# Two products on zeros between the score blocks of each group in batch 0

## The chip, the cores and the metric

The kernel runs on one core of one Trainium2 chip. The metric is the device time of one execution in microseconds; "before" is the median of four executions. A profiled execution has a span, from its first to its last instruction, and its own device time, which is a little longer.

## The reference

Attention over 8 batches of 12 heads (448 positions, 64 values a head), and then a two-layer network on its output.

```python
def _attn_ref(q, k, v):                       # each (8, 12, 448, 64)
    scores = q @ k.T / sqrt(64)
    attn = softmax(scores)
    return attn @ v

def _moe_ref(x, w_in, w_out):                 # x (3584, 768)
    h = x @ w_in                              # (3584, 2048)
    g = np.maximum(0.01 * h, h)
    return g @ w_out                          # (3584, 768)
```

## The kernel before

The work is cut into groups: a group `u` is two heads of one batch, so there are 48 groups, six to a batch (`HP` is 6). A group's path is this. `load` (line 91) fetches q, k and v; `cast` (104) turns them into bfloat16, on GpSimd except in group 0; `transposes` (164) turns q and k by eight TensorE products with the identity into PSUM (line 170), and VectorE copies them out (173). From group 12 on, a DMA does the turning.

`scores` (177) computes one block of 112 keys against all 448 queries, for both heads: two products of 64 rows into one slot of the pool `ps_s`. A group has four such blocks, c = 0 to 3. The pool has two slots, so that a block has to wait until the exponential of the block two before it has read its slot. `expo` (189) takes the exponential of a block on ScalarE (line 191), 112 partitions by 896 elements. `pv` (193) computes one head's product with v: 16 products (line 200) into the single slot of `ps_pv`, then a reciprocal (207) and a multiply (208) on VectorE. `x_transposes` (212) turns the result into `xT`, which the two-layer network reads.

`mlp` (236) is that network, over the tokens of one batch: products with `w_in` (line 243), the activation on ScalarE (248), products with `w_out` (260), a copy (265) and the store.

The order of the work is written out by hand: a schedule of eight slots for each group (`slots`, 306), in which each engine executes its instructions in the order in which they are issued. In slot 0 the first two blocks of scores are issued, in slot 2 the first head's `pv` of the group before, in slot 3 the transposes of the group after, in slot 4 the last two blocks, in slot 6 the second head's `pv` of the group before. For TensorE a steady group of batch 0 is therefore: blocks 0 and 1, the x transposes of two groups before, 16 pv products, 8 transposes, blocks 2 and 3, 16 pv products. Batch 0 (groups 0 to 5) has no network to run beside it. Group 6 has slots of its own (`turning_slots`, 271): it finishes batch 0 before it goes on. From slot 3 of group 6 on, the products of a batch's network are put between the slots of the next batch, in proportion.

`warm_up` (133) issues products of a tile of zeros with itself, 128 rows by 512 columns, each into a slot of `ps_mm`, the pool of two slots that the network uses later. Nothing reads what they write. Before, there are nine at the start (line 138), two after the first transposes (361) and four in slot 0 of group 0 (316), behind its two blocks.

Of the kernel before, what the change touches and what calls it, by code (L numbers as in the profile page):

```python
# [16 lines left out]
def kernel(  # L17
# [14 lines left out]
    HP = H // 2  # L32
# [58 lines left out]
    def load(u, queues=(nc.sync,) * 3):  # L91
        if u >= NU:
            return
        b, hp = divmod(u, HP)
        raw[u] = []
        for a, name, eng in zip((q, k, v), ("fq", "fk", "fv"), queues):
            t = ld_pool.tile([SC, 2, NSC, D], F32, name=name)
            eng.dma_start(
                out=t.rearrange("p h so d -> p h (so d)"),
                in_=a[b, 2 * hp:2 * hp + 2].rearrange("h (p so) d -> p h (so d)", so=NSC),  # L100
            )
            raw[u].append(t)

    def cast(u, by=(nc.gpsimd.tensor_copy,) * 3):
        if u >= NU:
            return
        fq, fk, fv = raw.pop(u)
        qk_sb[u] = cast_pool.tile([SC, 2, NSC, 2, D], BF16, name="qkb")
        by[0](qk_sb[u][:, 0].rearrange("p so h d -> p h so d"), fq)  # L109
        by[1](qk_sb[u][:, 1].rearrange("p so h d -> p h so d"), fk)  # L110
        by[2](v_sb[u % NV][:, :, :, :D], fv)  # L111
# [8 lines left out]
    def load_w(n=1):  # L120
        for _ in range(n):
            if w_steps:
                o, i = w_steps.pop(0)
                nc.gpsimd.dma_start(out=o, in_=i)  # L124
# [8 lines left out]
    def warm_up(n):  # L133
        for _ in range(n):
            ps = ps_mm.tile([P, 512], F32, name="mm")
            nc.tensor.matmul(ps, warm[:, :P], warm, start=True, stop=True)  # L136
# [23 lines left out]
    def dma_transposes(u):  # L160
        if NPE <= u < NU:
            turn(qkT[u % NQ][:, :QL], qk_sb[u].rearrange("p i so h d -> p (i so h d)"))

    def transposes(u):
        if u >= min(NPE, NU):
            return
        tr = ps_tr.tile([P, 2, S], BF16, name="tr")
        for i in range(2):
            for so in range(NSC):
                nc.tensor.transpose(  # L170
                    tr[:, i, ts(so, SC)], qk_sb[u][:, i, so], ident[:SC, :SC]
                )
        nc.vector.tensor_copy(qkT[u % NQ][:, :QL], tr.rearrange("p i s -> p (i s)"))  # L173
# [3 lines left out]
    def scores(u, c):  # L177
        ps = ps_s.tile([P, 2, 512], F32, name="sc")
        t = qkT[u % NQ]
        sc_t[u, c] = ps  # L180
        for j in range(2):
            nc.tensor.matmul(  # L182
                ps[:, j, :S],
                t[j * D:(j + 1) * D, S + c * SC:S + c * SC + P],
                t[j * D:(j + 1) * D, :S],
                start=True, stop=True,
            )

    def expo(u, c):
        e = e_sb[u % NE][:, :EL].rearrange("p (j c s) -> p j c s", j=2, c=NSC)  # L190
        nc.scalar.activation(e[:, :, c, :], sc_t.pop((u, c))[:SC, :, :S], AX.Exp, scale=scale)  # L191

    def pv(u, j):

        e, vt = e_sb[u % NE], v_sb[u % NV]
        ps = ps_pv.tile([P, NSC, D + 1], F32, name="pv")
        for qc in range(NSC):
            for c in range(NSC):
                at = (j * NSC + c) * S + qc * SC
                nc.tensor.matmul(  # L200
                    ps[:, qc, :], e[:, at:at + P], vt[:, j, c, :],
                    start=(c == 0), stop=(c == NSC - 1),
                )
        if j == 0:
            x_t[u] = x_pool.tile([SC, NSC, 2, D], BF16, name="x")
        rec = r_pool.tile([SC, NSC, 1], F32, name="rec")
        nc.vector.reciprocal(rec, ps[:SC, :, D:])  # L207
        nc.vector.tensor_mul(  # L208
            x_t[u][:, :, j, :], ps[:SC, :, :D], rec.to_broadcast([SC, NSC, D])
        )  # L210

    def x_transposes(u):
        b, hp = divmod(u, HP)
        at = b * S % NX
        dst = xT[:, hp, at:at + S]
        if u >= NPE - 3:
            turn(dst, x_t.pop(u).rearrange("p so h d -> p (so h d)"))
            return
        tr = ps_tr.tile([P, 2, S], BF16, name="tr")
        for so in range(NSC):  # L220
            nc.tensor.transpose(tr[:, 0, ts(so, SC)], x_t[u][:, so], ident[:SC, :SC])  # L221
        nc.vector.tensor_copy(dst, tr[:, 0, :])  # L222
# [83 lines left out]
    def slots(u):  # L306

        on = u < NU

        def s0():  # L310
            if on:
                scores(u, 0)
                scores(u, 1)
                expo(u, 0)
            if u == 0:
                warm_up(4)

        def s1():
            if on:
                expo(u, 1)  # L320
            if 2 <= u <= NU + 1 and u - 2 not in (HP - 2, HP - 1):
                x_transposes(u - 2)
            dma_transposes(u + 2)

        def s2():
            if 1 <= u <= NU:
                pv(u - 1, 0)

        def s3():
            load(u + 5)  # L330
            load_w({2: 1, 3: 2, 4: 2, 5: 2}.get(u, 0))
            if u + 1 < NU and u + 1 != HP:
                transposes(u + 1)

        def s4():
            if on:
                scores(u, 2)
                scores(u, 3)
                expo(u, 2)

        def s5():
            if on:
                expo(u, 3)
            cast(u + 3)

        def s6():
            if 1 <= u <= NU:
                pv(u - 1, 1)

        def s7():  # L350
            pass

        return [s0, s1, s2, s3, s4, s5, s6, s7]

    steps = [s for u in range(NU + 2) for s in (turning_slots if u == HP else slots)(u)]
# [53 lines left out]
```

## Time and profile before

| | |
|---|---|
| device time, median of 4 executions | 428.53 us (425.99 to 432.26) |
| the profiled execution, device time | 429.24 us |
| its span | 427.5 us |
| mean granted TensorE clock | 0.988 |
| score products (line 182) | 384, 55.0 us busy |
| exponentials (line 191) | 192, 168.1 us busy, 916 ns each |
| products on zeros (line 136) | 15, 5.3 us busy |

Batch 0 lies in the first 28 us or so of the profile, the turn to the dense part up to about 35 us; from there on TensorE has the network's products. "PE" is TensorE's products, "PEld" its weight loads, ACT ScalarE, DVE VectorE, POOL GpSimd. The granted clock is a share of full speed. [...]

### The profile page before, as it was taken

To read this page: it belongs to the slowest core of one execution; us is meant where nothing else is said; L and a number is where in the kernel's file an instruction comes from. 1 tells how busy PE (TensorE), PEld (TensorE's weight loads), DVE (VectorE), ACT (ScalarE), POOL (GpSimd) and SP (SyncE) were. 2 spreads that over 40 slices of the span, in tenths; PEclk is the share of its full clock that TensorE was granted. 3 is DMA by queue.
4 is the path that set the end of the run, shared out by engine and by line. 5 is a ranking of instruction groups with operands and counts; after the bars stand their busy time and mean duration, and the time that the engine had idled before them with its cause. 6 is when DMAs were issued, how large, how long until landed. Compare 5 with 4: busy or idle time off the path is not lost.

```text
span 427.5 us, 8982 instructions
## 1 busy us (share of the span) xinstructions
PE 414.3 (97%) x3716; PEld 227.8 (53%) x3731; DVE 100.3 (23%) x271; ACT 230.2 (54%) x322; POOL 92.5 (22%) x168
## 2 busy tenths in 40 slices
PE   7979999999999999999999999999999999999995
PEld 2654665544555555544455555554455555654563
DVE  1542333221132212221122212221123211320021
ACT  5875774566634676457644476456753477314300
POOL 5593323222111222211221131221112100000000
PEclk9897999999999999999999999999999999999999
DMA  8999999984655966675374966686445440230022
GB/s 230 264 250 244 250 248 203 239 222 109 110 143 156 203 135 172 177 185 139 97 146 126 184 181 136 183 189 157 127 100 135 115 93 13 60 85 2 0 75 74
DMA packets 98505, 63.66 MB, mean 149 GB/s; under 512 B 55456, under 2 KB 94880, under 8 KB 98464
## 3 DMA queue, kind: packets, MB, share of 16 engines
q1 hardware_dynamic: 90928, 56.56, 55.3%
q0 software_dynamic: 7296, 6.29, 9.3%
q8 instruction: 29, 0.48, 0.5%
q10 hardware_dynamic: 240, 0.23, 0.2%
q14 instruction: 12, 0.10, 0.1%
HBM read 45.61 MB, written 11.01 MB: 132 GB/s over the span
## 4 chain that ended last, share of the span: by engine, by line
PE 94%; ACT 2%; DMA 1%; issue 1%; POOL 1%; DVE 1%; SPq 0%; ACTq 0%
PE mm L243 35%; PE mm L260 35%; PE pv L200 11%; PE sc L182 10%; ACT e L191 2%; PE tr L170 1%; DMA fv<-in_v_dram 1%; PE tr L221 0%; POOL w_in_sb L124 0%; DVE x L208 0%; DVE qkT L173 0%; POOL qkb L109 0%; POOL v L111 0%; POOL qkb L110 0%; DVE o L265 0%
## 5 line engine op out<-in xcount | busy, mean ns | idle before, releaser
L191 ACT ACTIVATE e<-sc 112x896 bf16<-112x896 f32 x192 | 168.1, 916 | 109.9 <-PE sc L182 109.7
L243 PE MATMUL mm<-xT,w_in_sb 128*128 128x384 bf16 (+1 forms) x753 | 161.3, 354 | 0.8
L260 PE MATMUL mm<-w_out_sb,h 128*128 128x384 bf16 x896 | 160.7, 326 | 0.0
L260 PEld LDWEIGHTS <-h 128*128 128x128 bf16 x896 | 81.4, 98 | 62.3 <-issue 14.5
L243 PEld LDWEIGHTS <-w_in_sb 128*128 128x128 bf16 x768 | 68.5, 98 | 71.4 <-issue 17.5
L248 ACT ACTIVATE h<-mm 128x384 bf16<-128x384 f32 (+1 forms) x128 | 69.9, 546 | 59.0 <-PE mm L243 59.0
L111 POOL CAST v<-fv 112x512 bf16<-112x512 f32 x48 | 29.7, 619 | 202.2 <-PE pv L200 174.0
L200 PEld LDWEIGHTS <-e 112*128 112x128 bf16 x1536 | 61.8, 98 | 16.6 <-DVE x L208 2.0
L207 DVE RECIPROCAL rec<-pv 112x4 f32<-112x4 f32 x96 | 17.6, 183 | 212.1 <-PE pv L200 211.7
L200 PE MATMUL pv<-v,e 112*128 112x65 bf16 x1536 | 65.7, 195 | 1.4 <-DVE x L208 1.4
L182 PE MATMUL sc<-qkT 64*128 64x448 bf16 x384 | 55.0, 360 | 3.9 <-ACT e L191 2.8
L265 DVE COPY o<-mm 128x384 f32<-128x384 f32 x56 | 31.2, 557 | 86.6 <-PE mm L260 86.4
L208 DVE TENSOR_TENSOR x<-pv,rec 112x256 bf16<-112x256 f32 x96 | 40.8, 425 | 3.6 <-DVE rec L207 0.3
L109 POOL CAST qkb<-fq 112x512 bf16<-112x512 f32 x47 | 29.0, 618 | 33.6 <-DMA fq<-in_q_dram 16.7
L110 POOL CAST qkb<-fk 112x512 bf16<-112x512 f32 x47 | 29.0, 617 | 10.7 <-DMA fk<-in_k_dram 10.2
L182 PEld LDWEIGHTS <-qkT 64*128 64x128 bf16 x384 | 12.0, 94 | 35.9 <-issue 30.6
L173 DVE COPY qkT<-tr 128x896 bf16<-128x896 bf16 x12 | 7.5, 622 | 7.2 <-PE tr L170 7.0
L170 PE MATMUL tr<-ident,qkb 112*128 112x112 bf16 x96 | 8.2, 234 | 0.2
L170 PEld LDWEIGHTS <-qkb 112*128 112x128 bf16 x96 | 6.7, 109 | 2.3 <-DVE qkb L109 0.4
L136 PE MATMUL mm<-warm 128*128 128x512 bf16 x15 | 5.3, 501 | 1.2 <-DVE warm L131 1.2
L222 DVE COPY xT<-tr 128x448 bf16<-128x448 bf16 x9 | 3.5, 391 | 9.3 <-PE tr L221 9.3
L221 PE MATMUL tr<-ident,x 112*128 112x112 bf16 x36 | 3.5, 222 | 0.7 <-DVE qkT L173 0.7
(17 smaller groups left out, 15.1 us busy)
## 6 DMA issues: line engine op xcount, KB each, us to landing
fq<-in_q_dram SPq DMA_DIRECT2D x48, 224.0 KB, 3.9
fv<-in_v_dram SPq DMA_DIRECT2D x48, 224.0 KB, 4.1
fk<-in_k_dram SPq DMA_DIRECT2D x47, 224.0 KB, 3.7
w_in_sb<-in_moe_w_in_dram POOLq DMA_DIRECT2D x4, 768.0 KB, 14.1
w_out_sb<-in_moe_w_out_dram POOLq DMA_DIRECT2D x4, 768.0 KB, 34.1
out_dram<-o SPq DMA_DIRECT2D x8, 336.0 KB, 3.0
out_dram<-o SPq DMA_DIRECT2D x8, 288.0 KB, 2.7
out_dram<-o SPq DMA_DIRECT2D x8, 240.0 KB, 3.2
```

The costliest lines, as they stand in the source:

```text
L109: by[0](qk_sb[u][:, 0].rearrange("p so h d -> p h so d"), fq)
L110: by[1](qk_sb[u][:, 1].rearrange("p so h d -> p h so d"), fk)
L111: by[2](v_sb[u % NV][:, :, :, :D], fv)
L170: nc.tensor.transpose(tr[:, i, ts(so, SC)], qk_sb[u][:, i, so], ident[:SC, :SC])
L182: nc.tensor.matmul(ps[:, j, :S], t[j * D:(j + 1) * D, S + c * SC:S + c * SC + P], t[j * D:(j + 1) * D, :S], start=True, stop=True,)
L191: nc.scalar.activation(e[:, :, c, :], sc_t.pop((u, c))[:SC, :, :S], AX.Exp, scale=scale)
L200: nc.tensor.matmul(ps[:, qc, :], e[:, at:at + P], vt[:, j, c, :], start=(c == 0), stop=(c == NSC - 1),)
L208: nc.vector.tensor_mul(x_t[u][:, :, j, :], ps[:SC, :, :D], rec.to_broadcast([SC, NSC, D]))
L243: nc.tensor.matmul(ps[:, :n], w_in_sb[:, kk, ts(m, P)], xT[:, kk, at:at + n], start=(kk == 0), stop=(kk == KD - 1),)
L248: nc.scalar.activation(h[:, m, :n], ps[:, :n], AX.Prelu, alpha=0.01)
L260: nc.tensor.matmul(ps[:, :NW], h[:, m, ts(c, P)], w_out_sb[:, m, ts(w, NW)], start=(m == 0), stop=(m == MD - 1),)
L265: nc.vector.tensor_copy(o[c][:, ts(w, NW)], ps[:, :NW])
```

## The change

In slot 0 and in slot 4 of groups 0 to 5, two products on zeros are issued between the two blocks of scores. The four products on zeros at the end of slot 0 of group 0 are taken out. In all there are 35 products on zeros instead of 15.

```diff
         def s0():
             if on:
                 scores(u, 0)
+                if u < HP:
+                    warm_up(2)
                 scores(u, 1)
                 expo(u, 0)
-            if u == 0:
-                warm_up(4)
...
         def s4():
             if on:
                 scores(u, 2)
+                if u < HP:
+                    warm_up(2)
                 scores(u, 3)
                 expo(u, 2)
```

## The prediction

> **What bounds the kernel now.** I read the page's PE, clock and chain lines first, then the busy time in stretches of about 3.41 us, then PE's and ACT's rows in order of time for batch 0.
>
> ```profile
> PE 414.3 (97%) x3716; PEld 227.8 (53%) x3731; DVE 100.3 (23%) x271; ACT 230.2 (54%) x322; POOL 92.5 (22%) x168
> ...
> PEclk9897999999999999999999999999999999999999
> ...
> PE 94%; ACT 2%; DMA 1%; issue 1%; POOL 1%; DVE 1%; SPq 0%; ACTq 0%
> ```
>
> TensorE is busy 97% of the span and carries 94% of the chain, so a microsecond gained or lost ahead of the dense part, which begins near 35 us, should reach the end. The change touches only batch 0. What can be won there is waits and clock; the clock line is below 9 in two slices only, and the stretches show why (columns: stretch, its length, then the busy time of PE, PEld, DVE, ACT, POOL, then the granted clock, DMA share, GB/s):
>
> ```profile
> 7.68:11.10 3.42, 2.05 (x23) 1.00 (x22) 0.62 (x1) 3.01 (x4) 2.67 (x5) 1.00 1.13 273
> 11.10:14.50 3.40, 3.40 (x46) 2.41 (x43) 1.25 (x4) 2.45 (x4) 2.04 (x4) 0.50 1.17 243
> ...
> 24.74:28.15 3.41, 2.56 (x46) 1.74 (x44) 1.67 (x6) 3.40 (x5) 3.41 (x6) 1.00 1.19 246
> 28.15:31.56 3.41, 2.05 (x46) 1.59 (x46) 1.68 (x6) 1.61 (x2) 3.41 (x6) 1.00 1.17 242
> 31.56:34.97 3.41, 2.70 (x30) 1.66 (x27) 1.62 (x4) 0.20 (x1) 1.45 (x3) 0.50 1.18 244
> 34.97:38.39 3.42, 3.42 (x19) 1.75 (x19) 0.62 (x1) 2.02 (x3) 0.72 (x3) 0.50 1.18 249
> ```
>
> Twice a stretch in which PE was busy 2.05 us (60%) is followed by half clock: 3.4 us of it at the start of the groups, and 6.8 us at the turn from batch 0 to the dense part. A stretch with 2.56 us (75%) is not. So the limit lies between 60% and 75%. Now one steady group (start, duration, engine; in brackets the idle time before the row and what ended it):
>
> ```profile
> 20.35 0.55 PE L182 MATMUL sc<-qkT 64*128 64x448 bf16 x4
> 20.83 0.69 PE L200 MATMUL pv<-v,e 112*128 112x65 bf16 x16
> 21.78 0.36 PE L182 MATMUL sc<-qkT 64*128 64x448 bf16 x2 [0.26 <-DVE rec L207]
> 22.59 0.36 PE L182 MATMUL sc<-qkT 64*128 64x448 bf16 x2 [0.44 <-ACT e L191]
> 22.89 0.37 PE L221 MATMUL tr<-ident,x 112*128 112x112 bf16 x4
> 23.09 0.67 PE L200 MATMUL pv<-v,e 112*128 112x65 bf16 x16
> ...
> 20.81 3.34 ACT L191 ACTIVATE e<-sc 112x896 bf16<-112x896 f32 x4 [0.54 <-PE sc L182]
> ```
>
> The four exponentials take 3.34 us, ACT then idles 0.54 us until the third block's scores, and the next group's third block starts at 24.22: a group takes 3.88 us. Its cycle is: third block's scores (20.35), exponential at 20.81, the next one, then the slot for the next group's second block at 22.59, and 1.63 us of PE work up to 24.22. PE waits 0.44 us between the first and second block of a group. Between its third and fourth block it waits for nothing: both come in one row at 20.35.
>
> **The change part by part.** *The order.* PE gets 24 products in place of 4; DVE, ACT, POOL and SP keep their instructions and order, and no DMA is moved. The number of uses of the two mm slots stays odd (35 for 15), so the first real product meets the same slot.
>
> *Price of a pair at full clock.* From these rows (starts: second score pair 6.49, first zeros product 6.77, the third 7.22 as 6.77+2x0.22):
>
> ```profile
> 6.49 0.35 PE L182 MATMUL sc<-qkT 64*128 64x448 bf16 x2
> 6.77 0.61 PE L136 MATMUL mm<-warm 128*128 128x512 bf16 x2
> ...
> 6.77 1.04 PE L136 MATMUL mm<-warm 128*128 128x512 bf16 x4
> ...
> 7.65 0.84 PE L170 MATMUL tr<-ident,qkb 112*128 112x112 bf16 x8
> ```
>
> Four products fill 7.65-6.77 = 0.88 us, 0.22 each. From a score pair to the first zeros product is 0.28 us, where the next score pair would come after 0.20. So a pair moves the block behind it from 0.20 to 0.28+0.44 = 0.72 us: 0.52 us late unless PE would have waited anyway. The step back from zeros to scores has no row; zeros to transposes costs nothing beyond the 0.22, transposes to scores about 0.1 (0.145 against 0.05 between transposes). I take 0, the row after a zeros product being the nearer; the upper end is 0.1 per pair. Below nothing this step can't go.
>
> *Pair between first and second block (steady).* 21.78+0.28+0.44 = 22.50, and the slot comes at 22.59: hidden with 0.09 to spare, if the first block itself starts on time.
>
> *Pair between third and fourth block.* The fourth block goes from 20.55 to 21.07; its exponential starts at 21.63 and needs about 0.41 us from the scores' start (8.42 to 8.83 in another group): hidden. But the 16 products behind it start 0.52 late, at 21.35, and reach their last at 21.84 (0.49 in). The next first block then comes at about 21.98 instead of 21.78, its pair ends at 22.70, and the second block is 0.11 to 0.13 late. Everything up to the next third block follows, so a steady group takes 4.01 instead of 3.88. Who waits: the reciprocal and multiply behind these 16 products also come 0.52 later, at 22.30 to 22.72, ahead of the transposes of x at about 23.02; hidden.
>
> *First groups.* In group 0 the removed four ended at 7.65, where the transposes were waiting only for POOL's second cast half 0.5 us later; the new pair moves the second block to 7.02, and its exponential is due at 7.51: nothing. With the two new pairs, the stretch 7.68 to 11.10 gets 0.88 us more PE work, 2.9 of 3.42 us (86%), above the limit, so the half clock of 11.10 to 14.50 should go. Without it: second block of group 1 at 10.60 as now (its pair ends at 9.79+0.72 = 10.51), 16 products from 10.90 to 11.39, transposes to 11.90, third block at 12.04 instead of 12.52: 0.48 us won.
>
> *Sum up to the turn.* Third block of group 1: 12.04 (-0.48). Group 2: 12.04+4.01 = 16.05 (16.53 now, -0.48, since that cycle was slow already). Group 3: 20.06 (20.35, -0.29). Group 4: 24.07 (24.22, -0.15). Group 5, without transposes behind it: +3.35+0.13 = 27.55 (27.57, -0.02). There the fourth block now waits until 28.08 and would start at 28.27, so the 16 products behind it are 0.19 late, their multiply too, and the next ones, which wait for it (0.82 us at 29.89), start at 30.08. The turn is +0.19 us. Supplies are in time: the casts of group 4's q and k end at 18.02, wanted at about 19.5.
>
> *The turn.* No pair stands after 28.3. PE still waits 0.82, 0.54 and 0.71 us between 29 and 34 us, so the half clock of 31.56 to 38.39 stays.
>
> So 0.2 us more than the profiled execution's 429.24 us, which is its 427.5 span and 1.7 around it: 429.4. That execution is 0.7 above the median, 428.53. Executions in which the first drop doesn't happen have nothing to win and pay 0.19+0.48 = 0.67. I take the middle, 0.43, on the median: 429.0.
>
> [...] The trace has no PE wait longer than 0.82 us in the stretch before the first drop, and the clock halves all the same at 11.10. [...]
>
> **The rivals.**
> - *The turn keeps its clock too.* If the stretches fall otherwise over the waits of 0.82, 0.54 and 0.71 us, none may reach the limit. Half clock from 31.56 to 38.39: 16 products at 0.054 instead of 0.033 apart and 8 transposes about 0.7 together, x transposes and scores 0.55, seven products of 0.16 more each 1.1, eight transposes 0.4, scores 0.15: 2.9 us. Time 426.1. Against it: the waits lie on a chain of DVE and ACT which no pair fills.
> - *Zeros don't hold the clock.* The first drop stays, and two pairs fall into it: zeros products at half clock are 0.43 apart (nine in 3.62 us at the start), so 2x(0.86+0.1) = 1.9 us, with 0.6 from the later groups: 431.0. Against it: the same zeros precede full speed from 5.4 us on.
> - *Slower than 1%: half clock through batch 0.* If the clock falls at 11.1 and does not return until the turn, a group is PE's alone: 4 score pairs 1.5, 32 products 1.7, 12 transposes 1.1, four zeros 1.7, changes 0.5: 6.6 us against 3.9. Four groups cost 10.9: 439.4. It decides from 1.6 such groups. Against it: before, 3.4 us of full PE work brought the clock back at 14.50.
> - *It does nothing to be seen:* the second and fourth term cancel; this is what the main case amounts to.
>
> **How the numbers follow.** Main case 0.62 (429.0; own range 427.5 to 430.5: the 0.48 may be 0 to 0.75, the step back to scores adds up to 0.1 on each of nine pairs); turn keeps its clock 0.17; zeros don't hold it 0.16; half clock throughout 0.05. The four runs before spread from 425.99 to 432.26, so the range is 426.0 to 432.0, leaving out the last case and the tails. About 1% (4.3 us) is what a measurement of this kernel can tell from no change: faster by more 0.03, within 0.91, slower by more 0.06 (half clock throughout, and the tail of the third).
>
> **What would show it.** Right: full clock from 4.3 us to the turn; PE without waits of 0.44 in batch 0; third blocks 4.0 apart; fourth blocks 0.72 behind third ones; half clock only around 32 to 38 us. Wrong: half clock inside batch 0; groups over 4.2 us apart (then the step from zeros to scores costs more than taken); no half clock at the turn (then 426).

## The result, and the profile after

The changed kernel takes 429.52 us (median of 53 executions, 427.65 to 431.34) against 428.28 us before (79 executions, 425.94 to 432.26): the ratio is 1.0026, with a 95% interval of 1.0015 to 1.0037. So it is slower by about a quarter of a per cent, 1.1 us by the ratio.

The profiled execution of the changed kernel took 427.88 us with a span of 426.1, which is less than the profiled one before (429.24 and 427.5). That is chance, and the page's lines say what kind of chance:

```profile
PE 415.5 (98%) x3733; PEld 226.8 (53%) x3751; DVE 100.1 (23%) x271; ACT 230.7 (54%) x322; POOL 92.9 (22%) x168
...
PEclk9999999999999999999999999999999999999999
...
PE 96%; DMA 1%; DVE 1%; POOL 1%; issue 0%; ACT 0%; SPq 0%
```

No slice has half clock, neither in batch 0 nor at the turn. The one before had 10.2 us of it. A single pair of profiles therefore compares two draws of the clock as well as two kernels; the row of one steady group compares the kernels (PE in order of time, then ACT's row):

```profile
20.54 0.36 PE L182 MATMUL sc<-qkT 64*128 64x448 bf16 x2
21.06 0.38 PE L136 MATMUL mm<-warm 128*128 128x512 bf16 x1 [0.16 <-issue]
21.37 0.36 PE L182 MATMUL sc<-qkT 64*128 64x448 bf16 x2
21.66 0.69 PE L200 MATMUL pv<-v,e 112*128 112x65 bf16 x16
22.28 0.36 PE L182 MATMUL sc<-qkT 64*128 64x448 bf16 x2
22.58 0.61 PE L136 MATMUL mm<-warm 128*128 128x512 bf16 x2
23.11 0.36 PE L182 MATMUL sc<-qkT 64*128 64x448 bf16 x2
23.41 0.37 PE L221 MATMUL tr<-ident,x 112*128 112x112 bf16 x4
23.62 0.67 PE L200 MATMUL pv<-v,e 112*128 112x65 bf16 x16
...
24.75 0.36 PE L182 MATMUL sc<-qkT 64*128 64x448 bf16 x2
```

```profile
21.00 3.50 ACT L191 ACTIVATE e<-sc 112x896 bf16<-112x896 f32 x4 [0.72 <-PE sc L182]
```

The third block starts at 20.54 and the next one at 24.75: a group takes 4.21 us where it took 3.88. PE's waits for a slot are gone (the 0.16 ahead of 21.06 is where the record of the pair's first product is missing), and ACT now idles 0.72 us a group instead of 0.54, waiting for PE. PE has become the bound of batch 0. From block to block with a pair between is 0.83 us, at both places (20.54 to 21.37, 22.28 to 23.11), where the prediction had 0.72.

At the turn PE waits three times, 1.2 us later than in the profile before. First the kernel before, whose third wait fell into half clock, then the changed one:

```profile
29.89 0.67 PE L200 MATMUL pv<-v,e 112*128 112x65 bf16 x16 [0.82 <-DVE x L208]
...
31.30 0.89 PE L200 MATMUL pv<-v,e 112*128 112x65 bf16 x16 [0.54 <-DVE x L208]
...
33.65 0.53 PE L221 MATMUL tr<-ident,x 112*128 112x112 bf16 x4 [0.71 <-DVE qkT L173]
```

```profile
31.07 0.67 PE L200 MATMUL pv<-v,e 112*128 112x65 bf16 x16 [0.82 <-DVE x L208]
...
32.48 0.69 PE L200 MATMUL pv<-v,e 112*128 112x65 bf16 x16 [0.54 <-DVE x L208]
...
34.43 0.36 PE L221 MATMUL tr<-ident,x 112*128 112x112 bf16 x4 [0.87 <-DVE qkT L173]
```

The waits are still there, and yet these stretches, of which the last two are cut at the 3.41 us grid on which the clock changed (last section), show that the clock held this time (columns as in the prediction):

```profile
8.60:28.66 20.06, 19.41 (x253) 10.61 (x254) 9.30 (x26) 17.30 (x20) 13.16 (x21) 1.00 1.15 249
28.66:32.08 3.42, 2.45 (x42) 1.50 (x40) 1.36 (x6) 1.80 (x3) 3.42 (x6) 1.00 1.18 243
32.08:35.49 3.41, 2.14 (x34) 1.53 (x35) 2.17 (x6) 0.31 (x1) 2.06 (x4) 1.00 1.18 245
```

The grid here cuts the turn's waits into two stretches with PE busy 72% and 63%; in the profile before it put two of them into one stretch with 60%, and the clock fell.

The mean granted clock of each execution tells how often that happens. One stretch of 3.41 us at 0.50 takes 0.004 off the mean of a span of 426 us, so an execution at 0.996 or less is counted as one with half clock; 0.997 to 0.999 can come from the clock's fall behind the last product, which in this profile stands at 424.62 us and gives 0.998. Of the 54 executions of the changed kernel with a clock on record 29 had half clock, and none is under 0.989; of the 93 executions of the kernel before that were taken beside the experiments 70 had it, down to 0.988.

The price alone shows in the executions without half clock. The fastest are 427.65 and 425.95 us, 1.7 apart, but the medians are 428.06 (25 executions) and 427.54 (23), only 0.5 apart: those of the changed kernel lie between 427.65 and 428.89, those of the kernel before spread from 425.95 to 429.75, for a reason that is not the clock and that stays open. With half clock the medians are 430.25 and 428.58. So the changed kernel has half clock less often, but loses more to it where it has it. The mean of all executions lies above the mean of those without half clock by 1.1 us in the changed kernel and by 1.0 us in the one before: a gain from the clock in the sum is not shown.

### The profile page after: what moved, and what is told of

It is laid out like the page before. It is cut to its first block, busy times and chain, and to the rows that moved or that the text cites. A ratio compares the mean times of both kernels' runs of the same rounds, so it can differ in the third digit from the quotient of the medians.

```text
span 426.1 us, 9019 instructions
## 1 busy us (share of the span) xinstructions
PE 415.5 (98%) x3733; PEld 226.8 (53%) x3751; DVE 100.1 (23%) x271; ACT 230.7 (54%) x322; POOL 92.9 (22%) x168
## 4 chain that ended last, share of the span: by engine, by line
PE 96%; DMA 1%; DVE 1%; POOL 1%; issue 0%; ACT 0%; SPq 0%
PE mm L260 35%; PE mm L243 35%; PE pv L200 12%; PE sc L182 11%; PE mm L136 1%; PE tr L170 1%; DMA fv<-in_v_dram 1%; PE tr L221 1%; DVE x L208 0%; ACT e L191 0%; POOL w_in_sb L124 0%; POOL qkb L109 0%; POOL v L111 0%; DVE rec L207 0%; POOL qkb L110 0%
## 5 line engine op out<-in xcount | busy, mean ns | idle before, releaser
L136 PE MATMUL mm<-warm 128*128 128x512 bf16 x32 | 11.1, 448 | 1.7 <-DVE warm L131 1.2
L170 PE MATMUL tr<-ident,qkb 112*128 112x112 bf16 x96 | 7.0, 212 | 0.4 <-POOL qkb L109 0.2
L170 PEld LDWEIGHTS <-qkb 112*128 112x128 bf16 x96 | 5.7, 97 | 2.3 <-POOL qkb L109 0.5
L136 PEld LDWEIGHTS <-warm 128*128 128x128 bf16 x35 | 2.7, 109 | 5.5 <-issue 4.3
```

## The experiments

The theory: a pair between two blocks would mostly fit into the wait of a group if there were one, but two pairs together need more of PE than the waits hold, and each change between 64-row and 128-row products costs 0.09 us more than the products (in the changed kernel 0.29 us from a block to zeros and 0.31 from zeros to a block, where two blocks are 0.20 and two products on zeros 0.22 apart); what the clock gives back is less. The rivals: each pair costs its own time wherever it stands; the loss comes from taking the four products out; zeros do not hold the clock.

What the ten kernels gave, twelve executions each, beside the kernel before on the same chip:

| kernel | median us (lowest) | ratio to before, 95% interval | clock of 0.996 or less | steady groups apart, us |
|---|---|---|---|---|
| first pair alone | 428.82 (427.41) | 1.0013 (0.9990 to 1.0036) | 11 of 12 | 3.84 to 3.90 |
| second pair alone | 428.22 (426.50) | 1.0003 (0.9978 to 1.0028) | 6 | 3.88 to 3.90 |
| one product each | 427.94 (425.97) | 0.9992 (0.9969 to 1.0015) | 7 | 3.82 to 3.88 |
| the four removed, no pairs | 429.11 (426.44) | 1.0028 (1.0002 to 1.0054) | 9 | 3.82 to 3.88 |
| turn filled, batch 0 as before | 427.36 (426.25) | 0.9980 (0.9961 to 1.0000) | 5 | 3.82 to 3.88 |
| one product each, turn filled | 426.75 (425.89) | 0.9970 (0.9952 to 0.9988) | 0 | 3.82 to 3.88 |
| pairs of 64 rows | 427.41 (426.25) | 0.9989 (0.9966 to 1.0013) | 5 | 3.82 to 3.88 |
| pairs of 64 rows, turn filled | 426.67 (426.15) | 0.9976 (0.9956 to 0.9996) | 0 | 3.82 to 3.88 |
| the change, turn filled | 427.84 (427.49) | 0.9994 (0.9975 to 1.0012) | 0 | 4.21 |
| first pair alone, turn filled | 427.42 (426.01) | 0.9972 (0.9952 to 0.9992) | 0 | 3.84 and 4.08 |

The kernel before, beside them: 428.06 and 428.08 us (35 executions each, first four and next four rows), 427.91 us (23, last two).

**The first pair alone.**

```diff
 (against the changed kernel)
                 scores(u, 2)
-                if u < HP:
-                    warm_up(2)
                 scores(u, 3)
```

> Only the pair between the first and second block is kept (the four products of group 0 stay out). Theory (two pairs together outlast the waits, one does not): in the changed kernel a pair takes 0.83 us from one block to the next (0.29, 0.23, 0.31), and from a group's third block to the next group's second PE alone needs 0.83+0.29+0.62+0.83 = 2.57 us, where ACT's chain needs 2.24. With this pair alone PE needs 0.20+0.28+0.95+0.83 = 2.26: groups 3.88 to 3.90 us apart, not 4.21; fastest executions near 426.1 (as the fastest of before, 425.9), median near 427.5, below before, since the half clock inside batch 0 is gone. Rival (each pair costs its own time wherever it stands): half of the changed kernel's loss, groups 4.04 apart, fastest executions near 426.8.

The groups are 3.84 to 3.90 us apart: the theory's price, and not the rival's 4.04. The expected times failed: median 428.82, lowest 427.41, because 11 of 12 executions had half clock. In the profiled one it lies at the turn alone (from 31.44, for 6.83 us), after a stretch with PE busy 60%:

```profile
28.02:31.43 3.41, 2.05 (x54) 1.79 (x53) 1.51 (x5) 1.37 (x2) 3.41 (x6) 1.00 1.18 245
31.44:38.27 6.83, 6.11 (x40) 2.97 (x37) 2.25 (x5) 2.32 (x4) 2.64 (x5) 0.50 1.18 246
```

In this profile the pair held the clock in batch 0 (1.00 from 7.00 to 27.69 us) and could do nothing for the turn, which the last experiment tests.

**The second pair alone.**

```diff
 (against the changed kernel)
                 scores(u, 0)
-                if u < HP:
-                    warm_up(2)
                 scores(u, 1)
```

> Only the pair between the third and fourth block is kept (the four products of group 0 stay out). Theory: from a group's third block to the next first block PE needs 0.83+0.29+0.62 = 1.74 us, and the next second block still waits for its slot at 2.24: groups 3.88 us apart; in group 5 the fourth block comes 0.33 late and so does the turn; fastest executions near 426.3, median near 427.7. Rival (each pair costs its own time): groups 4.04 apart, fastest executions near 426.8.

PE in one steady group:

```profile
22.86 0.36 PE L182 MATMUL sc<-qkT 64*128 64x448 bf16 x2
23.38 0.38 PE L136 MATMUL mm<-warm 128*128 128x512 bf16 x1 [0.16 <-issue]
23.70 0.36 PE L182 MATMUL sc<-qkT 64*128 64x448 bf16 x2
23.99 0.69 PE L200 MATMUL pv<-v,e 112*128 112x65 bf16 x16
24.61 0.36 PE L182 MATMUL sc<-qkT 64*128 64x448 bf16 x2
25.13 0.37 PE L182 MATMUL sc<-qkT 64*128 64x448 bf16 x2 [0.16 <-ACT e L191]
...
26.77 0.36 PE L182 MATMUL sc<-qkT 64*128 64x448 bf16 x2
```

The pair (the record of its first product is missing here too) takes its 0.84 us and pushes the 16 products and the first block, but PE still waits 0.16 us for the slot of the second block at 25.13, so the group takes 3.90. Alone, neither pair costs a steady group anything to speak of; together they cost 0.33. The two share one stock of waiting time, which the first of them to come uses up. The lowest time, 426.50, and the median, 428.22, lie somewhat over the expected 426.3 and 427.7.

**One product at each place.**

```diff
 (against the changed kernel, at both places)
-                    warm_up(2)
+                    warm_up(1)
```

> One product on zeros in place of two at both places (the four of group 0 stay out). Theory: a block, one product and the next block take 0.29+0.31 = 0.60 us, so PE needs 0.60+0.29+0.62+0.60 = 2.11 us, under the 2.24 of ACT's chain: groups 3.88 us apart, fastest executions near 426.1, median 427.0 to 427.6. Rival (what counts is the number of changes between products of 64 and 128 rows, four in a group as in the changed kernel): groups over 4.0 apart, fastest executions over 426.7.

Groups 3.82 to 3.88 apart and a lowest time of 425.97: the theory's price, and not the rival's. The median, 427.94, missed the expected 427.6, with half clock in 7 of the 12 executions. Four changes of row count in a group remain, and they fit. Half clock inside batch 0 is gone from the profile; at the turn there are 3.4 us of it.

**The four products taken out, no pairs.**

```diff
 (against the kernel before)
                 expo(u, 0)
-            if u == 0:
-                warm_up(4)
```

> Only the removal of the four products of group 0, no pair anywhere. Theory: the removal moves nothing, since the transposes behind the four wait for POOL's cast until 8.1 us anyway: fastest executions 426.0, median 428.3 to 428.8, half clock inside batch 0 in about as many executions as before. Rival (the changed kernel's loss comes from the removal, through an earlier or longer half clock): median 429.3 or more.

Here the theory's part failed: median 429.11, 0.28% above before. The removal does not delay the order of the work: the third block of group 0 comes 2.41 us after the first (9.12 and 6.71), as in the profile of the filled turn, which has the four (9.07 and 6.66). The clock is what changes. As many executions have half clock as before (9 of 12, before 27 of 35), but it can last longer: the mean clock goes down to 0.981, where it was 0.988. In the profiled execution the stretch in which the four products stood comes out at 60%, and two stretches of half clock follow:

```profile
5.37:8.78 3.41, 2.04 (x20) 0.79 (x18) 0.62 (x1) 1.86 (x3) 2.68 (x4) 1.00 1.12 231
8.78:15.60 6.82, 5.93 (x58) 3.23 (x58) 1.86 (x4) 4.68 (x7) 3.88 (x7) 0.50 1.15 237
```

The second pair alone, which lacks a product between the first two blocks, shows the same (2.04 us busy in 6.18 to 9.59, then half clock to 16.42). By these two profiles the four did hold the clock, and in the changed kernel it is the pair between the first two blocks of group 0 that takes their place. The rival (that the removal explains the loss of the changed kernel) falls all the same: the fastest execution here is 426.44, far below 427.65, and the groups of the changed kernel are long in full clock.

**The turn filled, batch 0 as before.**

```diff
 (against the kernel before, in turning_slots)
         def s0():
+            warm_up(4)
             pv(u - 1, 0)
...
         def s1():
+            warm_up(3)
             pv(u - 1, 1)
...
         def s2():
+            warm_up(4)
             x_transposes(u - 1)
```

> The kernel before, and products on zeros in the three waits of the turn of batch 0 alone: four ahead of the first 16 products, three ahead of the second 16, four ahead of the x transposes (0.22 us each: 0.88 in a distance of 1.02 us, 0.65 in 0.75, 0.88 in 1.08). Theory (zeros in a wait cost nothing and hold the clock): the half clock at the turn, some 2.9 us where it comes, is gone from nearly all executions, that inside batch 0 stays; fastest executions 426.0, median 426.3 to 427.3. Rival (the half clock at the turn does not come from these waits, or zeros do not count): median 428 as before.

Median 427.36, just outside the theory's 426.3 to 427.3, ratio 0.9980 (0.9961 to 1.0000). Five of twelve executions still have half clock, none under 0.994 (before: 11 of 35 at 0.992 or less); in the profile it is one stretch, from 11.41 to 14.83, inside batch 0. The zeros in the waits of the turn held the clock there. The five executions with half clock have a median of 427.49, the seven without 426.93: inside batch 0 it cost some 0.6 us, by few executions.

**One product at each place, and the turn filled.** The two edits above together.

> One product on zeros at each of the two places in batch 0, and zeros in the three waits of the turn. Theory: no half clock from the first groups to the end in nearly all executions, and no lost time: fastest 425.9 to 426.1, median 426.0 to 426.7, below both kernels. Rival (zeros do not hold the clock): median 427.9 as with one product each.

PE at the turn:

```profile
28.12 0.69 PE L200 MATMUL pv<-v,e 112*128 112x65 bf16 x16
28.87 0.81 PE L136 MATMUL mm<-warm 128*128 128x512 bf16 x3
29.55 0.68 PE L200 MATMUL pv<-v,e 112*128 112x65 bf16 x16
30.07 0.36 PE L221 MATMUL tr<-ident,x 112*128 112x112 bf16 x4
30.26 0.81 PE L136 MATMUL mm<-warm 128*128 128x512 bf16 x3
30.96 0.67 PE L200 MATMUL pv<-v,e 112*128 112x65 bf16 x16
31.47 0.56 PE L170 MATMUL tr<-ident,qkb 112*128 112x112 bf16 x8
31.86 1.03 PE L136 MATMUL mm<-warm 128*128 128x512 bf16 x4
32.90 0.36 PE L221 MATMUL tr<-ident,x 112*128 112x112 bf16 x4
```

The first row of zeros shows three of the four; the record of one is missing. Where PE waited 0.82, 0.54 and 0.71 us, it now works, and the products behind the zeros are not late. No execution had a mean clock under 0.997. The median is 426.75, just above what was expected; the ratio of 0.9970 (0.9952 to 0.9988) is the lowest here, though its interval overlaps those of the kernels with 64-row pairs or the first pair and a filled turn; it is faster than the one before and than the changed one.

**Pairs of 64 rows.**

```diff
 (against the changed kernel)
-    def warm_up(n):
+    def warm_up(n, rows=P):
...
-            nc.tensor.matmul(ps, warm[:, :P], warm, start=True, stop=True)
+            nc.tensor.matmul(ps, warm[:rows, :P], warm[:rows], start=True, stop=True)
...
 (at both places in batch 0)
-                    warm_up(2)
+                    warm_up(2, D)
```

> The changed kernel with pairs of 64 rows in place of 128 (the same 512 columns, the same time in the array). [...] For the clock: if 64 rows count as work as 128 do, as few half-clock executions as with the changed kernel.

If the lost time goes with the change of row count, 0.63 to 0.66 us from block to block was expected, groups 3.88 us apart and a fastest execution of 426.0 to 426.3; if not, the changed kernel's 0.83, 4.21 and 427.7.

```profile
19.92 0.36 PE L182 MATMUL sc<-qkT 64*128 64x448 bf16 x2
20.12 0.38 PE L136 MATMUL mm<-warm 64*128 64x512 bf16 x1
20.12 0.35 PE L182 MATMUL sc<-qkT 64*128 64x448 bf16 x1
20.34 0.38 PE L136 MATMUL mm<-warm 64*128 64x512 bf16 x1
20.55 0.35 PE L182 MATMUL sc<-qkT 64*128 64x448 bf16 x1
20.83 0.68 PE L200 MATMUL pv<-v,e 112*128 112x65 bf16 x16
...
23.80 0.36 PE L182 MATMUL sc<-qkT 64*128 64x448 bf16 x2
```

Both products of the third block start at 19.92. The first product on zeros starts 0.20 later; beside it, on the other 64 rows, runs already one product of the fourth block, and the other one comes at 20.55, behind the zeros: 0.63 us from block to block instead of 0.83, with the same columns in line on the rows that the zeros use. Groups are 3.88 apart again. So the lost 0.2 us goes with the two changes of row count and not with the number of products, the tile or the wait. The lowest time is 426.25, 1.4 us below that of the changed kernel.

**Pairs of 64 rows, and the turn filled.** The two edits together.

> Pairs of 64 rows in batch 0, and 128-row zeros in the three waits of the turn. Theory: as with one product each and the turn, no lost time and no half clock: median 426.0 to 426.7. If 64-row products count less for the clock, half clock inside batch 0 remains in some executions, median 426.5 to 427.5.

Median 426.67, no execution of the twelve with half clock: here products of 64 rows held the clock in batch 0 as well.

**The change, and the turn filled.** The changed kernel with the three fillings of the turn.

> The changed kernel, and products on zeros in the three waits of the turn (four, three and four). Theory: the changed kernel is its fastest executions (427.65) wherever no half clock falls, and what lies above 429 is the half clock at the turn; with that filled, all executions lie between 427.6 and 429.0, median near 428.2, none with a mean clock of 0.996 or less, where the changed kernel had 29 of 54. Rival (the executions above 429 come from half clock inside batch 0, in the longer groups): still about half of the executions above 429.

All twelve executions lie between 427.49 and 428.31, none with half clock, median 427.84. This is the changed kernel without its chance: what lay above 429 was half clock at the turn, and the price of the pairs stays. Against the two kernels above that have the turn filled and groups of 3.82 to 3.88 us, and no half clock either (on a chip where the kernel before took 428.08 us, here 427.91), it is 1.1 us by the medians (427.84 against 426.75 and 426.67) and 1.3 to 1.6 us by the lowest.

**The first pair alone, and the turn filled.**

> The pair between the first and second block alone, and products on zeros in the three waits of the turn. Theory: the median of the first pair alone, 428.8, was high because the half clock at the turn fell into 11 of its 12 executions; with the turn filled the fastest execution is 426.0 to 426.3 and the median 426.6 to 427.0, as with one product each. Rival (the pair costs time of its own): fastest 427.4 as before, or the 0.85 of half the changed kernel's loss, 426.8.

No half clock, and a lowest time of 426.01 as expected: in its best case the pair has no price of its own, and the 427.41 of the first experiment was the clock. The median, 427.42, missed the 427.0; it is close to the 427.54 of the kernel before without half clock. In the profiled execution one group took 4.08 us in full clock, and the rows show what came late:

```profile
21.25 0.62 POOL L111 CAST v<-fv 112x512 bf16<-112x512 f32 x1 [2.10 <-DMA fv<-in_v_dram]
...
22.62 0.62 POOL L109 CAST qkb<-fq 112x512 bf16<-112x512 f32 x1
...
23.17 0.62 POOL L110 CAST qkb<-fk 112x512 bf16<-112x512 f32 x1
...
23.84 0.21 PEld L170 LDWEIGHTS <-qkb 112*128 112x128 bf16 x4 [0.16 <-POOL qkb L110]
```

POOL waited 2.10 us for a load of v, so its casts of q and k for the next group ended at 23.79, and the transposes waited for them. Here the supply of data was next in line. Whether late loads explain the whole spread of these executions (up to 429.58 at full mean clock), and that of the kernel before, stays open.

## Why the prediction was right or wrong

*The size.* 429.0 was forecast, 0.5 above before, and 429.52 was measured, 1.1 to 1.2 above. Same sign, and within 1%. That it is so close is in part luck: the price between undisturbed executions was taken 1.0 us too small (0.67 for 1.7), and the kernel before is seldom as fast as its undisturbed rows.

*The step that failed: the way back from zeros to scores.* The prediction took 0 for it, by the zeros-to-transposes row, and kept 0.1 as the upper end, from the transposes-to-scores row. It measured 0.09 to 0.1: zeros to the next block 0.31 instead of 0.22, a pair 0.83 instead of 0.72. Groups over 4.2 us apart were the prediction's own sign for this, and they came. The row with the like change of row count was the right neighbour, not the row that began with the like product. With PE already the bound, the two such steps of each group went straight into the time: 4.21 instead of 4.01 a group, over three groups and parts of others, some 0.8 us. The rows of the undisturbed sum: third blocks at 8.60, 12.11, 16.32, 20.54, 24.75 and 28.44, where the kernel with one product each, at full clock, has 8.58, 12.06, 15.88, 19.69, 23.57 and 26.92. That is 1.5 us, and 0.2 more up to the products behind the last fourth block: the 1.7 between the fastest executions, where the prediction had 0.67.

*Each pair hidden or not.* Right in kind. The first pair was said to be hidden if the first block starts on time, the second to push that block; each pair alone left the groups at 3.84 to 3.90, both together made PE the bound.

*The clock in batch 0.* Right: full clock from 4.8 us to the turn in the profile, in the stretch that fell before too, and with the turn filled as well no half clock in 12 executions, where the filled turn without pairs left it in 5 of 12. The rival that zeros do not hold the clock is refuted: the four kernels with zeros in batch 0 and at the turn had half clock in none of 48 executions, the kernel before in 70 of 93. As in the prediction's sum, the gain in batch 0 (0.48 there, some 0.6 by the filled turn) does not outweigh the price.

*The four products of group 0.* Costed at nothing, since the transposes wait for POOL anyway. True of the order, wrong of the clock: without them and without pairs the median rose by 0.28%. In the change the new pair covers it, so the sum did not suffer.

*The turn.* "The half clock of 31.56 to 38.39 stays" is wrong as a statement on one execution; it comes in about half of them. The rival that gave it 2.9 us had the right size: 430.3 to 431.3 where the mean clock is 0.992 or less, as with two stretches, 429.5 to 430.4 at 0.995 or 0.996, as with one, and 427.7 to 428.9 with none. It is a draw for every execution, not a case for the kernel, and belongs into the range rather than among the rivals.

*The waits and the limit.* No wait of PE in batch 0 or at the turn was longer than 0.82 us in the profile before, whose clock fell at 11.10 and 31.58 us, or than 0.87 in the changed kernel's, whose clock held there. What went with the drops was a busy share of 60% or less in a 3.41 us stretch, and filling the turn's waits of 0.5 to 0.9 us ended them there. The limit between 60% and 75% that the prediction read from its stretches holds for these only: at the end of the kernels 46% was enough (last section). Where the grid lies differs between profiles: the clock first rose at 4.1 to 7.2 us in the twelve (4.27 before, 4.78 in the changed kernel), and in the two profiles shown where the grid cut the turn went with its half clock: 60% in one stretch and a fall before, 72% and 63% and no fall after.

## What to carry to other kernels

A filler in a wait is free only as long as all fillers between two releases of the same slot, with the changes of row count that they bring, stay below the wait that they share; sum them along the cycle, not one by one. Match the filler's rows to its neighbours' (here 0.63 us from block to block with equal rows, 0.83 with unequal ones), and put it where the busy share of a 3.41 us stretch is lowest, here the turn, rather than where there are most waits. Where the clock makes executions differ by 3 us, sort them by it: compare those without half clock, by their medians as well as their fastest, for the price, and for the gain both how many have half clock and what it costs them.

## What the runs showed of the hardware

- The clock changed only on a grid of 3.41 us: in the kernel before at 4.27, 11.10, 14.51, 31.58 and 38.40 us, which are 2, 1, 5 and 2 times 3.41 apart. In batch 0 and at the turn a fall followed stretches with PE busy 53% to 60% (2.04 and 2.05 us of 3.41 in five of them: two of the kernel before, and one each of the first pair alone, the second pair alone and the four removed); stretches of 63% and more never led to one (2.14 us of 3.41 at the changed kernel's turn), and two near the limit (2.06 us of 3.42 with pairs of 64 rows, 2.00 of 3.41 with the second pair alone) did not either.
- These 60% belong to the products of batch 0 and the turn, not to busy time as such. At the end of the kernels, where PE has products of 128 rows and 384 columns, stretches with 46% to 57% kept the clock and two with 39% lost it. The first two lines are from the first pair alone, the last two from the change with the turn filled:

```profile
420.56:423.97 3.41, 1.56 (x10) 0.72 (x8) 0.56 (x1) 0.00 (x0) 0.00 (x0) 1.00 0.08 14
423.97:427.38 3.41, 0.00 (x0) 0.00 (x0) 0.00 (x0) 0.00 (x0) 0.00 (x0) 1.00 0.33 101
...
419.92:423.33 3.41, 1.34 (x9) 0.59 (x6) 0.56 (x1) 0.00 (x0) 0.00 (x0) 1.00 0.13 30
423.33:426.27 2.94, 0.00 (x0) 0.00 (x0) 0.00 (x0) 0.00 (x0) 0.00 (x0) 0.50 0.32 99
```

- An estimate sorts both kinds of stretch: count each product with 0.42 ns a column (products on zeros of 512 columns start as little as 0.216 us apart) times its share of 128 rows. In the twelve profiles, from the first rise on, all 20 falls then follow stretches with at most 38.1%, and all stretches that kept it but one (36.9%) have at least 38.6%; the two falls of the kernel before follow 35% and 36%, and the changed kernel's turn, where the clock held, has 45%. It was fitted afterwards, and no run tests it; what the clock counts stays open.
- At half clock, a stretch with 74%, 79% or 81% of busy time did not bring full clock back (79% is the 2.70 us of 3.41 from 31.56 in the kernel before); one with 90% (3.08 us of 3.41, up to the rise at 4.27 there) and filled ones (up to 14.51 and 38.40) did.
- Between products of 64 rows and of 112 or 128 rows PE lost about 0.09 us in each direction (0.29 and 0.31 us between starts for 0.20 and 0.22); between two of 128 rows (0.22 us apart), or two blocks of 64 (0.20), nothing. What PE does in the 0.09 us was not shown. With all rows the same, loads ran beside a product: in the kernel before products on zeros start at 6.77, 7.00, 7.22 and 7.43 and last 0.38 to 0.39 us each, and the loads of 0.10 us start at 6.78, 7.00 and 7.22; with pairs of 64 rows the load for the first zeros starts at 19.93, while the block's product on the same rows, begun at 19.92, runs. At a change between 64 and 128 rows, where a load lasts 0.09 to 0.10 us as well, it starts only with its product (21.36 and 21.37 in the changed kernel). Whether the load takes the 0.09 us, or PE stops at the change and the load comes behind, these rows do not tell.
